# Windowed attention and a token/channel mixer on one core: the last tile's normalised x ahead of a weight conversion's second half, and two parts of u split in one go

## The chip, the core and the metric

The kernel runs on one core of a Trainium2 chip. The metric is the device time of one execution in microseconds (us). Five engines work side by side: TensorE (PE in the profile; PEld is its loading of weights), VectorE (DVE), ScalarE (ACT), GpSimd (POOL) and SyncE (SP), which here does nothing but start transfers. Each engine goes through its own instructions in order; they wait for one another through semaphores. ACT and SP both start DMAs.

## What is computed

Attention in a window of 64 positions, its heads put side by side as x, then a token mixing and a channel mixing with a skip each. All is float32:

```python
# q, k, v: (8, 8, 576, 64)
scores = q @ k^T / 8;  kept where 0 <= row - column < 64, else -1e9
attn   = softmax(scores);  x = (attn @ v) as (8, 576, 512)
h  = relu(x^T @ w_tok1) @ w_tok2        # (576,256), (256,576)
u  = x + h^T
out = u + relu(u @ w_ch1) @ w_ch2       # (512,1536), (1536,512)
```

The weights come as float64.

## The kernel before

**Stages.** The attention stage has 36 tiles, numbered i = 0 to 35 (NT = 36), each with two blocks of 64 rows of all eight heads. For each tile TensorE makes the scores (`qk`), DVE masks them, ACT takes the exponential, TensorE transposes (`pt_transpose`) and multiplies with v (`av`, into the PSUM tile xp), and DVE multiplies xp with the reciprocal sums (`norm`, L355), which gives x of the tile, such as x35. The token mixing is laid between the tiles: `split_x` casts x to a rounded high part xhi on ACT and subtracts to a low part xlo on POOL (L117), `tok1` multiplies both with w_tok1 (into h, L386), `finish_h` and `finish_h_low` make hhi (ACT, L400) and hlo (DVE, L409), and `tok2`, one of the "pieces", makes one of four column parts of u for one of two halves of a batch (up6_1_3 is batch 6, half 1, part 3; L430 and L437). ACT copies each piece from PSUM (L442) into a buffer u (two buffers, u7_1 takes that of u6_1), and after the fourth part a store (L457) brings it to u_dram. The last stores are started by ACT, all others by SP.

After the attention come three stretches of the channel mixing over nine chunks of 512 tokens. The first, on chunk 0, multiplies u with w_ch1 (`gemm1`, PSUM tile gp, L667). `load_u` loads u of a chunk from u_dram (tile uf, L124); for chunk 0 these are four loads on SP, one for each part. `split_u` makes of each part uhi on ACT (L114) and ulo on DVE (L117). One gp tile is twelve products of 512 columns, three for each part of u.

**The weights.** A job is the conversion of a float64 piece of a weight of 384 columns to float32 in DVE's integer arithmetic. `job_convert_a` issues its first half on DVE (L215, L217, L218, tile c). `job_convert_b` issues the second half: L227 and L229 on DVE, then L230 into tile r (one buffer), and one addition on POOL (L232) into tile w (two buffers). For the pieces of w_ch2 that are converted in the attention stage `job_finish` then stores w to w2_dram on SP (L270). Tile 35 has two jobs, 29 and 30.

**What sets the order.** Nothing is rescheduled: each engine's row is the order in which the Python code issues. The table JOBS gives the number of jobs of each tile, PIECES the number of pieces before and behind `av`. In tile 35 the loads of chunk 0's u are issued at the end, behind the stores of the last two jobs. Iteration 36 holds tok1 of x35 and two pieces; the loop over the four parts of u behind it runs the last eight pieces, of batch 7, two with each part. At the end the pieces go in turn to the PSUM tags "up" (one bank), "s" and "pt" (two banks each); "s" and "pt" are gp's tags too.

Of the kernel before, what the change touches and what calls it, by code (L numbers as in the profile page):

```python
# [28 lines left out]
NT = NPAIR * TPP  # L29
DT = 256  # L30
F = 1536
NCT = C // P
# [16 lines left out]
N_START = 7  # L49
# [46 lines left out]
def mixer_kernel(ctx: ExitStack, tc: tile.TileContext, qh, kh, vh, wt1, wt2, wc1, wc2, out):  # L96
# [15 lines left out]
    def split(eng_hi, eng_lo, hi, lo, src):  # L112
        if eng_hi is nc.scalar:
            nc.scalar.copy(hi, src)  # L114
        else:
            eng_hi.tensor_copy(hi, src)
        eng_lo.tensor_sub(lo, src, hi.bitcast(F32))  # L117
# [9 lines left out]
    def split_u(u, cts=range(NCT)):  # L127
        uf, uhi, ulo = u
        for ct in cts:
            split(nc.scalar, nc.vector, uhi[:, ct], ulo[:, ct], uf[:, ct])  # L130
# [5 lines left out]
    with ExitStack() as actx:  # L136
# [8 lines left out]
        def load_k(i):  # L145
            p, t = divmod(i, TPP)
            if t in (0, 4):
                b = 2 * p + (t == 4)
                kbs[b] = pq.tile([P, NBLK + 1, H // 2, BLK], F32, name=f"k{b}", tag="k", bufs=2)
                if b != 0:  # L150
                    nc.sync.dma_start(kbs[b], kh[b])

        def load_q(i):
            qr = pq.tile([P, H // 2, 2, BLK], F32, name=f"q{i}", tag="q", bufs=5)
            nc.sync.dma_start(qr, qh[i])
            loaded[i] = [qr, None]

        def load_v(i):
            vt = pq.tile([P, 2, H, D], F32, name=f"v{i}", tag="v", bufs=3)
            nc.sync.dma_start(vt, vh[i])  # L160
            loaded[i][1] = vt
# [102 lines left out]
        def job_finish():  # L264
            if to_finish:
                n, w = to_finish.pop(0)
                finished.add(n)
                src, hi, lo, o, m = jobs[n]
                if hi is None:
                    nc.sync.dma_start(w2_dram[:, o:o + m], w)  # L270
                else:
                    eng = nc.vector if n >= N_FIRST else nc.gpsimd
                    split(nc.scalar, eng, hi[:, o:o + m], lo[:, o:o + m], w)
                    if src is wt1 and o + m == 5 * DT:
                        for c, r in enumerate((top, bottom)):
                            nc.gpsimd.tensor_copy(t1z[r, c], t1lo[r, 4 * DT:].bitcast(F32))
# [24 lines left out]
        def softmax(i, part):  # L301
            if part == 0:
                st[i] = (pa.tile([P, H], F32, name=f"nm{i}", tag="nm", bufs=3),
                         pa.tile([P, H], F32, name=f"sum{i}", tag="sum", bufs=3))
            nm, sm = st[i]
            mk = mask[1 if tile_blocks(i)[0][1] == 0 else 0]
            for u, h in heads(i, part):
                if (i, u) not in e_sb:
                    e_sb[i, u] = pa.tile([P, 4, P], F32, name=f"e{i}_{u}", tag="e", bufs=4)
                g = 2 * h + u  # L310
                nc.vector.tensor_tensor_reduce(out=e_sb[i, u][:, h], in0=s_ps[i][h // 2 * 2 + u][:, h], in1=mk,  # L311
                                               scale=-scale, scalar=MAX_F32, op0=ALU.add, op1=ALU.min,
                                               accum_out=nm[:, g:g + 1])
# [8 lines left out]
        def pt_transpose(i, u):  # L322
            pp = ps.tile([P, 4, P], F32, name=f"pp{i}_{u}", tag="pt")
            e = e_sb.pop((i, u))
            for h in range(4):
                nc.tensor.transpose(pp[:, h], e[:, h], ident)  # L326
            pt = pa.tile([P, 4, P], F32, name=f"pt{i}_{u}", tag="ptsb", bufs=4)
            nc.scalar.copy(pt, pp)  # L328
            return pt
# [13 lines left out]
        def recip(i):  # L343
            _, sm = st.pop(i)
            ri = pa.tile([P, H], F32, name=f"ri{i}", tag="ri", bufs=2)
            if i < N_START:
                nc.gpsimd.tensor_scalar_add(ri, sm, 1e-9)
            else:
                nc.vector.scalar_tensor_tensor(out=ri, in0=sm, scalar=1e-9, in1=sm, op0=ALU.add, op1=ALU.max)
            nc.vector.reciprocal(ri, ri)  # L350
            return ri
# [98 lines left out]
        def store_u():  # L450
            while stores:
                us, g0, n = stores.pop(0)
                a = 0
                while a < n:
                    j, o = divmod(g0 + a, CHUNK)
                    m = min(n - a, CHUNK - o)
                    (nc.sync if g0 < (B - 1) * S - 320 else nc.scalar).dma_start(u_dram[j][:, :, o:o + m], us[:, :, a:a + m])  # L457
                    a += m
# [16 lines left out]
        def run_pieces(k):  # L475
            for _ in range(min(k, len(pieces))):
                tok2(*pieces.pop(0))
# [23 lines left out]
        for i in range(-1, NT + 1):  # L501
            if 0 <= i and i + 2 < NT:
                load_v(i + 2)
            if 3 <= i + 3 < NT:
                load_q(i + 3)
            if i + 4 < NT:
                load_k(i + 4)
            store_u()
            n_jobs = JOBS[i]
            if i == NT - 1:  # L510
                up_tags += [("s", 2), ("pt", 2)]
            have = len(pieces)
            n_pieces = PIECES.get(i, (1, 1) if i >= TOK2_FROM else (0, 0))
            pts = []
            if 0 <= i < NT:
                pts.append(pt_transpose(i, 0))
                if i < NT - 1:
                    pts.append(pt_transpose(i, 1))
            if i + 1 < NT:
                softmax(i + 1, 0)  # L520
            if i + 1 < NT:
                softmax(i + 1, 1)
            if 0 <= i < NT:
                ri = recip(i)
            if i >= N_START:
                while to_finish:
                    job_finish()
            for n in tok1_plan.get(i + 1, ()):
                last_use = n - NX + ((n - NX) % TPP == 4)
                if n < i and last_use not in tok1_plan.get(i, ()):  # L530
                    split_x(n)
            if i + 1 < NT:
                softmax_exp(i + 1, 0)
            while to_finish:
                job_finish()
            run_pieces(min(have, n_pieces[0]))
            have = min(have, len(pieces))
            if i >= N_START:
                for _ in range(n_jobs):
                    job_convert_a()  # L540
            if i == NT - 1:
                pts.append(pt_transpose(i, 1))
            if i < N_START:
                softmax_exp(i + 1, 1)
            late = i - 1 if i in BEHIND else NT
            for n in tok1_plan.get(i, ()):
                if n < late:
                    tok1(n)
            if N_START <= i < NT - 1:
                softmax_exp(i + 1, 1)  # L550
            if i >= N_START:
                for _ in range(n_jobs):
                    job_convert_b()
            if i == 0:
                job_convert_a()
            if 0 <= i < NT:
                norm(i, av(i, pts), ri)
            finish_h_low()
            if i < N_START:
                for _ in range(n_jobs):  # L560
                    if i > 0:
                        job_convert_a()
                    job_convert_b()
            if i + 2 < NT:
                qk(i + 2)
            if late in tok1_plan.get(i, ()):
                tok1(late)
                finish_h_low()
            if to_convert and N_ABS <= to_convert[0][0] < N_APART and JOBS[i + 1]:
                job_abs()  # L570
            for n in tok1_plan.get(i + 1, ()):
                if n not in xhl:
                    split_x(n)
            run_pieces(min(have, n_pieces[1]))
            while to_load and len(to_convert) < 2 and i < NT - 1:
                job_load()
            if i == NT - 1:
                while to_convert or to_convert_b or to_finish:
                    job_convert_a()
                    job_convert_b()  # L580
                    job_finish()
                qctx.close()
                pu = uctx.enter_context(tc.tile_pool(name="pu", bufs=1, side="right", reuse_waits="tile"))
                ul = {0: load_u(0, pu)}
        for ct in range(NCT):
            split_u(ul[0], (ct,))
            run_pieces(2)
        assert not pieces

# [708 lines left out]
```

## Time and profile before

| | us |
|---|---|
| median of 3 runs | 794.13 (793.02 to 794.43) |
| the profiled execution's own time | 792.06 |
| its span, from the first to the last instruction | 790.3 |
| TensorE busy within the span | 776.4 (98%) |
| DVE, ACT, POOL busy | 591.4, 403.8, 340.2 |

The span lies 1.8 us under the execution's own time; what lies around it is start and end. The granted clock of TensorE was 1.00 in the whole span. A row of a timeline reads: start, duration, engine, line, operation, output and inputs, shapes, and in brackets how long the engine stood idle before it and what ended that. A row of the chain reads: start, duration, what the end of the program hung on in that time.

### The profile page before, as it was taken

The page shows a single profiled execution, that of the slowest core. Times are in us where ns is not written, and L with a number is a line of the kernel's source. Part 1 is how long each engine was busy: PE and PEld are TensorE (multiplying, and loading weights), DVE is VectorE, ACT ScalarE, POOL GpSimd, SP SyncE. Part 2 cuts the span into 40 slices and gives each one's busy share as a digit, 9 for nine tenths or more (in the row PEclk, how much of TensorE's full clock was granted, in tenths as well). Part 3 has the DMA queues.
Part 4 walks back from the last instruction along what each step waited for, and adds up shares of the span by engine and source line. Part 5 has one row for each costly group of instructions (what it writes and reads, how often), then busy time and mean ns, then how long its engine had stood idle before and what let it go on. Part 6 is the DMA issues. An engine that isn't in the chain of part 4 may idle for free.

```text
span 790.3 us, 15910 instructions
## 1 busy us (share of the span) xinstructions
PE 776.4 (98%) x5713; PEld 647.6 (82%) x5713; DVE 591.4 (75%) x1547; ACT 403.8 (51%) x1151; POOL 340.2 (43%) x298
## 2 busy tenths in 40 slices
PE   8999999999999999999999899999999999999997
PEld 6778888888888888888888688888888888888886
DVE  6998889689883987777897866667766667757576
ACT  7999979989864532454425332234323144414040
POOL 4654445444331001025758631549722648723140
PEclk9999999999999999999999999999999999999999
DMA  9866769767847669994979575765975856955533
GB/s 348 309 238 231 240 212 311 257 208 275 280 142 243 191 196 291 287 291 153 304 237 367 197 304 202 264 244 176 330 273 187 294 186 238 345 197 200 199 152 107
DMA packets 88976, 191.76 MB, mean 243 GB/s; under 512 B 9024, under 2 KB 52800, under 8 KB 86976
## 3 DMA queue, kind: packets, MB, share of 16 engines
q1 hardware_dynamic: 86784, 188.90, 69.1%
q10 hardware_dynamic: 2112, 1.84, 0.7%
q8 instruction: 45, 0.74, 0.4%
q14 instruction: 35, 0.29, 0.1%
HBM read 148.24 MB, written 42.47 MB: 241 GB/s over the span
## 4 chain that ended last, share of the span: by engine, by line
PE 66%; DVE 2%; DMA 1%; issue 1%; ACT 0%; POOL 0%; DVEq 0%; POOLq 0%; ACTq 0%
PE op L1109 22%; PE gp L1047 21%; PE gp L667 12%; PE op L675 4%; DMA u_dram<-u 1%; DVE m L904 0%; PE op-1_0_1_3_5769 L1109 0%; PE op-1_1_1_3_6046 L1109 0%; PE op-1_2_1_2_6335 L1109 0%; PE op-1_2_1_0_6333 L1109 0%; PE op-1_2_1_3_6336 L1109 0%; PE op-1_2_0_2_6259 L1109 0%; PE op-1_2_0_3_6260 L1109 0%; PE op-1_2_0_0_6257 L1109 0%; PE op-1_1_1_2_6045 L1109 0%
## 5 line engine op out<-in xcount | busy, mean ns | idle before, releaser
L1047 PE MATMUL gp<-m,w1hi 128*128 128x512 f32 x504 | 155.3, 389 | 2.7 <-DVE x L1056 2.7
L319 ACT ACTIVATE e<-e,nm 128x128 f32<-128x128 f32 x288 | 112.3, 398 | 4.7 <-DVE nm L311 4.7
L1047 PEld LDWEIGHTS gp<-m,w1hi 128*128 128x128 f32 x504 | 94.5, 188 | 22.7 <-DVE x L1056 3.1
L1047 PE MATMUL gp<-m,w1lo 128*128 128x512 f32 x252 | 98.0, 389 | 0.0
L1098 DVE TENSOR_TENSOR uf<-op,uf 128x512 f32<-128x512 f32 (+1 forms) x91 | 61.9, 683 | 39.7 <-PE op L1109 31.9
L117 POOL TENSOR_TENSOR m7lo<-t3g,m7hi 128x512 fp32r<-128x512 f32 x18 | 23.4, 1300 | 148.9 <-ACT m7hi L114 148.9
L311 DVE CUSTOM_DVE_ANT_0 e<-s,mask 128x128 f32<-128x128 f32 x288 | 63.6, 286 | 10.2 <-PE s L292 10.1
L232 POOL TENSOR_TENSOR w<-r,c 128x384 f32<-128x384 f32 (+1 forms) x31 | 30.9, 995 | 67.1 <-DVE r L230 56.1
L667 PE MATMUL gp<-ulo,w1hi 128*128 128x512 f32 x144 | 56.1, 390 | 0.2 <-DVE ulo L117 0.2
L319 ACT ACTIVATION_READ_ACCUMULATOR e<-e,nm 128x1 f32 x288 | 56.2, 195 | 0.0
L667 PE MATMUL gp<-uhi,w1hi 128*128 128x512 f32 x144 | 56.1, 390 | 0.0
L667 PE MATMUL gp<-uhi,w1lo 128*128 128x512 f32 x144 | 56.0, 389 | 0.0
L1047 PEld LDWEIGHTS gp<-m,w1lo 128*128 128x128 f32 x252 | 47.3, 188 | 9.8
L117 POOL TENSOR_TENSOR xlo<-x,xhi 128x512 fp32r<-128x512 f32 x32 | 41.1, 1285 | 29.0 <-ACT xhi L114 28.7
L1050 ACT COPY x<-gp 128x512 f32<-128x512 f32 x18 | 10.6, 588 | 75.3 <-PE gp L1047 75.3
L338 PEld LDWEIGHTS xp<-v,pt 128*64 128x64 f32 x1152 | 36.7, 138 | 13.5 <-ACT e L319 9.0
L292 PE MATMUL s<-k,q 64*64 64x128 f32 x1152 | 40.8, 275 | 2.8 <-DMA q<-qh 1.6
L437 PE MATMUL up<-t2hi,hhi 128*128 128x320 f32 (+1 forms) x128 | 43.0, 336 | 0.0
L338 PE MATMUL xp<-v,pt 128*64 128x64 f32 x1152 | 41.7, 225 | 1.1 <-ACT pt L328 0.8
L326 PE MATMUL pp<-ident,e 128*128 128x128 f32 x288 | 40.9, 277 | 0.5
L328 ACT COPY pt<-pp 128x512 f32<-128x512 f32 x72 | 38.9, 587 | 2.7 <-PE pp L326 1.1
L437 PE MATMUL up<-t2hi,hlo 128*128 128x320 f32 (+1 forms) x128 | 37.8, 296 | 0.0
(477 smaller groups left out, 2146.7 us busy)
## 6 DMA issues: line engine op xcount, KB each, us to landing
v<-vh SPq DMA_DIRECT2D x36, 512.0 KB, 4.3
w1hi<-w1s SPq DMA_DIRECT2D x18, 896.0 KB, 5.2
w1lo<-w1s SPq DMA_DIRECT2D x18, 896.0 KB, 6.9
w1hi<-w2s SPq DMA_DIRECT2D x18, 896.0 KB, 4.5
w1lo<-w2s SPq DMA_DIRECT2D x18, 896.0 KB, 6.4
raw<-wc SPq DMA_DIRECT2D x32, 384.0 KB, 5.2
q<-qh SPq DMA_DIRECT2D x36, 256.0 KB, 4.9
k<-kh SPq DMA_DIRECT2D x7, 1280.0 KB, 8.3
```

Source lines behind the costliest of these rows:

```text
L117: eng_lo.tensor_sub(lo, src, hi.bitcast(F32))
L292: nc.tensor.matmul(so, qt[r, j, half], kbs[b][r, n:n + 2, j], start=True, stop=True)
L311: nc.vector.tensor_tensor_reduce(out=e_sb[i, u][:, h], in0=s_ps[i][h // 2 * 2 + u][:, h], in1=mk, scale=-scale, scalar=MAX_F32, op0=ALU.ad ...
L319: nc.scalar.activation(e[:, h], e[:, h], AF.Exp, bias=nm[:, g:g + 1], scale=-1.0, accum_out=sm[:, g:g + 1])
L326: nc.tensor.transpose(pp[:, h], e[:, h], ident)
L328: nc.scalar.copy(pt, pp)
L338: nc.tensor.matmul(xp[half * BLK:(half + 1) * BLK, h], pts[h % 2][:, h // 2, half * BLK:(half + 1) * BLK], vt[:, half, h], start=True, sto ...
L437: nc.tensor.matmul(up[:, :n], hx[:, cs], w[:, tt * S + s0:tt * S + s0 + n], start=False, stop=(k == 6), skip_group_check=True)
L667: nc.tensor.matmul(gp, w[:, w1_at(ft, ct)], x[:, ct], start=(k == 0), stop=(k == 3 * NCT - 1))
L1047: nc.tensor.matmul(b[INTO[m]], w[:, at], c[:, h, t], start=(k < 4 and z == y == 0), stop=(z == 1 and y == 2), skip_group_check=True)
L1098: eng.tensor_add(x, y, x)
L1109: nc.tensor.matmul(bank[:, cols], w[:, o:o + P], x[:, cols], start=(i == 0 and y == 0 and m in ("m1", "m6", "m7", "m5")), stop=(i == 1 and ...
```

## The change

Two edits. In the last tile (i = 35) the second half of the conversion jobs is no longer issued ahead of `av` and `norm`; it falls to the loop that already closes the tile, which drains all jobs, so it comes behind x35 and the split of x35. And the fourth part of chunk 0's u is split directly behind the third, ahead of the two pieces that stood between them; the last two pieces come behind both.

```diff
             if N_START <= i < NT - 1:
                 softmax_exp(i + 1, 1)
-            if i >= N_START:
+            if N_START <= i < NT - 1:
                 for _ in range(n_jobs):
                     job_convert_b()
...
-        for ct in range(NCT):
-            split_u(ul[0], (ct,))
+        for cts in ((0,), (1,), (2, 3), ()):
+            split_u(ul[0], cts)
             run_pieces(2)
```

How the rows of the engines move. In the rows the first number of a name is that of the tile or the job, the last one is only a running number. DVE, in tile 35, behind the first halves of jobs 29 and 30:

```order
 L218 TENSOR_SCALAR c30_4382<-c30_4382 128x384
+L355 TENSOR_TENSOR x35_4416<-xp35_4399,ri35_4330 128x512
 L227 SCALAR_TENSOR_TENSOR c29_4378<-raw29_4230,c29_4378 128x384
-L229 TENSOR_SCALAR r29_4399<-c29_4378 128x384
-L230 SCALAR_TENSOR_TENSOR r29_4399<-raw29_4230,r29_4399 128x384
+L229 TENSOR_SCALAR r29_4422<-c29_4378 128x384
+L230 SCALAR_TENSOR_TENSOR r29_4422<-raw29_4230,r29_4422 128x384
 L227 SCALAR_TENSOR_TENSOR c30_4382<-raw30_4321,c30_4382 128x384
-L229 TENSOR_SCALAR r30_4405<-c30_4382 128x384
-L230 SCALAR_TENSOR_TENSOR r30_4405<-raw30_4321,r30_4405 128x384
-L355 TENSOR_TENSOR x35_4428<-xp35_4411,ri35_4330 128x512
+L229 TENSOR_SCALAR r30_4429<-c30_4382 128x384
```

x35 moved from behind six instructions to ahead of them; hlo7_0 and hlo7_1 follow behind r30 in both. POOL, at the same place:

```order
-L232 TENSOR_TENSOR w29_4400<-r29_4399,c29_4378 128x384
-L232 TENSOR_TENSOR w30_4406<-r30_4405,c30_4382 128x384
-L117 TENSOR_TENSOR xlo35_4431<-x35_4428,xhi35_4430 128x512
+L117 TENSOR_TENSOR xlo35_4419<-x35_4416,xhi35_4418 128x512
+L232 TENSOR_TENSOR w29_4423<-r29_4422,c29_4378 128x384
+L232 TENSOR_TENSOR w30_4430<-r30_4429,c30_4382 128x384
```

xlo35 moved past both additions. SP's row is the same before and after, and stands here for what follows the stores of w29 and w30 (this is the changed kernel's):

```order
L270 DMA w2_dram_68<-w29_4423 128x384
L270 DMA w2_dram_68<-w30_4430 128x384
L124 DMA uf0_4440<-u_dram0_73 128x512 x4
L247 DMA raw31_4617<-wc2 128x384
L247 DMA raw32_4619<-wc2 128x384
```

The four loads of chunk 0's u stay behind both stores. ACT at the second edit, before:

```order
L114 CAST uhi0_4441<-uf0_4440 128x512
L442 COPY u7_0_4506<-up7_0_0_4497 128x256
L442 COPY u7_0_4506<-up7_0_1_4508 128x256
L114 CAST uhi0_4441<-uf0_4440 128x512
L442 COPY u7_0_4506<-up7_0_2_4520 128x256
L442 COPY u7_0_4506<-up7_0_3_4530 128x256
L457 DMA u_dram7_80<-u7_0_4506 512x1x64
L457 DMA u_dram8_81<-u7_0_4506 512x1x192
L114 CAST uhi0_4441<-uf0_4440 128x512
L442 COPY u7_1_4554<-up7_1_0_4544 128x320
L442 COPY u7_1_4554<-up7_1_1_4556 128x320
L114 CAST uhi0_4441<-uf0_4440 128x512
```

and in the changed kernel, from the second of these stores on:

```order
L457 DMA u_dram8_81<-u7_0_4506 512x1x192
L114 CAST uhi0_4441<-uf0_4440 128x512 x2
L442 COPY u7_1_4556<-up7_1_0_4546 128x320
L442 COPY u7_1_4556<-up7_1_1_4558 128x320
L442 COPY u7_1_4556<-up7_1_2_4569 128x320
L442 COPY u7_1_4556<-up7_1_3_4580 128x320
```

The fourth cast moved past two copies, and those past it. TensorE's row has the same products in the same order before and after.

## The prediction

> **What bounds the kernel now.** I read the page first (span, busy shares, chain), then the chain in order of time, then the engines' timelines and the DMA issues around the one place where the chain leaves TensorE for long.
>
> ```profile
> span 790.3 us, 15910 instructions
> PE 776.4 (98%) x5713; PEld 647.6 (82%) x5713; DVE 591.4 (75%) x1547; ACT 403.8 (51%) x1151; POOL 340.2 (43%) x298
> PE 66%; DVE 2%; DMA 1%; issue 1%; ACT 0%; POOL 0%; DVEq 0%; POOLq 0%; ACTq 0%
> ```
>
> TensorE is busy for 98% of the span, so a change elsewhere counts only where it opens or closes a hole in TensorE's row. The chain in order of time shows such a hole at the end of the attention stage:
>
> ```profile
> 236.12 1.01 POOL w L232
> ...
> 237.38 1.28 POOL xlo L117
> ...
> 238.70 1.42 PE h L386 x5
> ...
> 241.37 0.43 ACT u L442
> ...
> 241.82 8.69 DMA u_dram<-u
> ...
> 251.34 0.53 ACT uhi L114
> ...
> 251.90 0.70 DVE ulo L117
> ...
> 252.64 30.67 PE gp L667 x134
> 283.31 32.64 PE op L675 x144
> ```
>
> The reader is to see two things. TensorE's tok1 product of the last tile (h, 238.70) was held by POOL's xlo, and xlo stands behind a weight's w. Then TensorE's first channel product (gp) was held by the fourth part of chunk 0's u (uhi, ulo), which ScalarE reached late because two copies ahead of it had to wait for a store. From 252.64 on TensorE runs without a hole for over 60 us, so what is won or lost before it reaches the end one to one; the later stages keep their distance from it, since what they wait for is made from its products.
>
> **Edit 1: x35 ahead of the conversion's second half.** The rows of DVE, TensorE, ACT and POOL at that place:
>
> ```profile
> 234.09 1.15 PE L338 MATMUL xp<-v,pt 128*64 128x64 f32 x32
> 233.59 0.55 DVE L227 SCALAR_TENSOR_TENSOR c<-raw,c 128x384 int32<-128x384 int32 x1
> 235.03 0.36 DVE L229 TENSOR_SCALAR r<-c 128x384 int32<-128x384 int32 x1 [0.89 <-POOL w L232]
> 235.43 0.56 DVE L230 SCALAR_TENSOR_TENSOR r<-raw,r 128x384 f32<-128x384 uint32 x1
> 235.91 0.68 DVE L355 TENSOR_TENSOR x<-xp,ri 128x512 f32<-128x512 f32 x1
> 236.68 0.62 ACT L114 CAST xhi<-x 128x512 fp32r<-128x512 f32 x1 [3.29 <-DVE x L355]
> 233.81 1.19 POOL L232 TENSOR_TENSOR w<-r,c 128x384 f32<-128x384 f32 x1 [3.26 <-DVE r L230]
> 236.12 1.01 POOL L232 TENSOR_TENSOR w<-r,c 128x384 f32<-128x384 f32 x1 [1.12 <-issue]
> 237.37 1.28 POOL L117 TENSOR_TENSOR xlo<-x,xhi 128x512 fp32r<-128x512 f32 x1 [0.24 <-ACT xhi L114]
> 237.65 0.40 PE L386 MATMUL h<-xhi,t1hi 128*128 128x512 f32 x1
> ```
>
> xp35 is there at 234.09 + 1.15 = 235.24, and x35 began only at 235.91, behind r30. With x35 first it begins at about 235.28, 0.63 earlier; xhi35 follows at 236.05, xlo35 on POOL (0.69 behind xhi, as before) from 236.74 to 238.02, and the waiting product h at 238.06 instead of 238.70. That is 0.64 us gained at this point. The first h product, at 237.65, does not move, and little of the hole is left behind it.
>
> Now what went behind x35. Two jobs (29 and 30) each have L227, L229 and L230 on DVE, one w on POOL and one store on SP. DVE starts job 29's L227 at 235.94, and its L229 runs from 236.50 to 236.86. L230 then meets xlo35 on POOL (from 236.74). What this costs, two older rows show:
>
> ```profile
> 77.84 1.20 POOL L117 TENSOR_TENSOR w1lo<-w,w1hi 128x384 fp32r<-128x384 f32 x1 [0.95 <-ACT w1hi L114]
> 78.21 1.25 DVE L227 SCALAR_TENSOR_TENSOR c<-raw,c 128x384 int32<-128x384 int32 x1
> ```
>
> A DVE instruction of L230's form, 0.55 alone, took 1.25 beside a POOL subtraction and ended 0.42 after it (79.46 against 79.04). So L230 ends at 238.02 + 0.42 = 238.44, 1.0 later than free. [...]
>
> From there: w29 starts 0.13 after r29 (235.99 to 236.12 in job 30's rows), at 238.57, and takes 1.19 as it did beside job 30's L227: 239.76. r has one buffer, so job 30's L229 waits for w29, as its bracket (0.89) shows, and w30 starts 1.09 after that L229 (235.03 to 236.12): 240.88, ending at 241.89. Before, w30 ended at 237.13. It is 4.76 later.
>
> DVE's hlo7, now behind r30 in DVE's row, would begin at 240.7 instead of 240.11; it costs TensorE a few tenths ahead of the larger wait below and is swallowed by it.
>
> **What stands behind w30 on SP.** Its store to w2_dram, and behind the store the four loads of chunk 0's u:
>
> ```profile
> 237.16 0.33 SPq L270 DMA_DIRECT2D w_dram<-w  x1
> 237.54 0.42 SPq L124 DMA_DIRECT2D uf<-u_dram  x1
> 241.44 1.62 SPq L247 DMA_DIRECT2D raw<-wc  x3
> uf<-u_dram SPq DMA_DIRECT2D x1, 256.0 KB, 3.8
> ```
>
> SP issues in order, so the first load moves from 237.54 to 242.30. The edit that hastens x35 delays data that the last copies stand behind. The landing has no row at its new place. The lower bound is the load's own row, 3.8, taken when little else moved. The upper one comes from a load that ran beside the 640 KB store of ACT:
>
> ```profile
> raw<-wc SPq DMA_DIRECT2D x1, 384.0 KB, 4.9
> u_dram<-u ACTq DMA_DIRECT2D x1, 640.0 KB, 8.7
> u_dram<-u ACTq DMA_DIRECT2D x1, 640.0 KB, 3.5
> ```
>
> The first two are neighbours (the first of SP's three raw loads at 241.44, and the store at 241.82), the third is the last such store, with less beside it. Now the 8.7 us store goes out at about 241.18, 0.64 earlier, and the loads of u come at 242.30, beside its larger part. I take the middle of 3.8 and 4.9, 4.35: the first part of u lands at 246.65. [...]
>
> **Who waits for uf.** ACT's row, and TensorE's:
>
> ```profile
> 242.52 0.62 ACT L114 CAST uhi<-uf 128x512 fp32r<-128x512 f32 x1 [0.73 <-ACT u L442]
> 244.17 0.37 ACT L442 COPY u<-up 128x256 f32<-128x256 f32 x1
> 246.80 0.62 ACT L114 CAST uhi<-uf 128x512 fp32r<-128x512 f32 x1 [1.33 <-issue]
> 246.11 0.38 PE L430 MATMUL up<-ident,x 128*128 128x128 f32 x2
> 249.72 0.39 PE L667 MATMUL gp<-uhi,w1hi 128*128 128x512 f32 x1
> 253.22 0.39 PE L667 MATMUL gp<-uhi,w1hi 128*128 128x512 f32 x1
> 255.95 0.39 PE L667 MATMUL gp<-uhi,w1hi 128*128 128x512 f32 x1
> ```
>
> The first uhi did not wait for uf before (its bracket names ACT's own copy). Now ACT stops at it until 246.7. Behind it on ACT stand the copies of up7_0_0 to up7_0_2. The bank "up" has one buffer; up7_1_1 (246.11 on TensorE) takes it after up7_0_2, whose copy ended at 244.17 + 0.37 = 244.54: 1.57 us of slack. Now that copy ends 2.02 after the first uhi's start (242.52 to 244.54): 248.72, and up7_1_1 starts at 248.76, 2.65 late. All three products up to gp are late by that.
>
> **Edit 2: the fourth part with the third.** The first gp group took from 249.72 to 253.22, 3.50; the next took 2.73 (to 255.95). The 0.77 between them is the wait for the fourth uhi and ulo. With both casts together, the fourth uhi no longer stands behind two copies that wait for the store. The third uhi starts at most 2.63 behind the copy of up7_0_2 (244.17 to 246.80), by 250.98, so the fourth ulo is done by 253.0 (two casts of 0.62, then 0.7); it is needed after ten products of 0.23, at 252.37 + 2.3 = 254.6. The 0.77 goes. The four copies of up7_1 (0.4 each) come behind both casts, until about 253.8; the second gp group, which takes the bank of up7_1_0, starts at 255.1, so they are covered. Without that cover they would cost a cast's length, 0.6.
>
> **Sum.** +2.65 − 0.77 = +1.88 us: 0.64 is won at h, lost at the bank, and the loss is larger than both wins. By the ends of the landing, +1.3 (3.8) to +2.4 (4.9). The profiled execution (792.06, span 790.3) would take 793.9; the median of the runs lies 2.07 above it, at 794.13, which gives 796.0.
>
> **Rivals.**
> 1. Small cost: L230 gets by before xlo35, or the loads land at 3.8. w30 then ends about 0.7 earlier, and the two together leave +0.3 to +1.3. For it: L229 and xlo35 start only 0.24 us apart. Against: L230 comes after xlo35's start by my times, and POOL's rows never let it go early. Time 794.4 to 795.4.
> 2. Not slower: the late loads don't reach TensorE. It decides at the bank "up": if the first part lands by about 244.0 (246.11 less 2.02, and a little), no copy holds up7_1_1 and both wins stay: −0.64 − 0.77 = −1.4, so 792.7. The load would have to land within 1.7 us of its issue, or w30 would have to end by 239.8. The rows of SP and POOL speak against it.
> 3. Heavier contention: the loads and the store meet in full. The raw loads behind the first took longer (a row below); at 6.9 the sum is +4.4, 798.5; at the store's own 8.7 it is +6.2.
>
> ```profile
> raw<-wc SPq DMA_DIRECT2D x1, 384.0 KB, 6.9
> ```
>
> Against it: raw moves half as much again, and the three raw loads themselves now wait.
>
> **How the numbers follow.** 0.2%, 1.59 us, is about what a measurement of this kernel can tell from no change (its runs span 793.02 to 794.43). Late loads as summed 0.60, two thirds of it above 1.59 (0.40 slower, 0.20 same); small cost 0.16 (same); not slower 0.10 (0.04 of it beyond −1.59 with the runs' spread, else same); heavier contention 0.14 (slower). Slower 0.54, same 0.42, faster 0.04. The likeliest case is 796.0, its own range 795.4 to 796.5. The range goes from the small cost's 794.4 less the 1.1 by which a run lies under the median, 793.2, to 798.6, the 6.9 us landing: it leaves out the full gain and the far tail.
>
> **What would show it.** Right: x35 ahead of L227 on DVE, h with next to no wait for xlo, L230 stretched to over 1 us, w30 ending near 241.9, SP's uf loads from about 242.3, the first uhi waiting for DMA uf, TensorE waiting for ACT's u copy ahead of an up product by 2 to 3 us, and no wait for ulo within gp. Wrong: uf loads issued ahead of 240, or no hole of TensorE between 240 and 250; or TensorE's later stages taking the shift up, if one of them is held by something that did not move.

## The result: slower, by more than twice the forecast

The changed kernel takes 798.77 us (median, 798.58 to 799.0), the kernel before on the same chip 793.58 (791.45 to 794.43): a ratio of 1.0073, 95% interval 1.0054 to 1.0091, or +5.2 us. Forecast were 796.0 and +1.9. The place, the sign and the chain of waits are those of the prediction; the size is not, and one cause, TensorE's clock, was not in it. The profiled execution took 799.0, its span is 797.2 (before 790.3).

The chain of the changed kernel in order of time, at the end of the attention stage:

```profile
240.74 1.01 POOL w L232
...
241.76 0.33 SPq L270
...
242.14 5.76 DMA uf<-u_dram
...
248.51 0.64 ACT u L442 x2
249.15 0.52 ACT uhi L114
249.66 0.28 ACT u L442
249.94 0.04 issue
249.99 0.55 PE up L430 x3
250.54 1.12 PE up L437 x6
251.66 0.64 PE up L430 x3
252.30 1.60 PE up L437 x6
...
255.41 32.66 PE gp L667 x144
...
452.27 15.51 PE gp L1047 x60
```

It no longer passes through xlo35 and the store of u. It passes through the second addition w30, that weight's store on SP, the first load of chunk 0's u behind it, ACT's copies behind the first cast, and only then TensorE. Two things in it were not in the forecast. The load takes 5.76, not 4.35. And two equal pieces of TensorE's work (three L430 and six L437 each) take 0.55 + 1.12 and then 0.64 + 1.60. The second is slower although it waits for nothing.

TensorE's timeline at the hole shows why; the bracket is the idle time ahead of a row:

```profile
245.95 0.31 PE L437 MATMUL up<-t2hi,hlo 128*128 128x320 f32 x1
249.99 0.44 PE L430 MATMUL up<-ident,x 128*128 128x128 f32 x2 [3.73 <-ACT u L442]
...
250.67 0.31 PE L437 MATMUL up<-t2hi,hlo 128*128 128x320 f32 x1
250.81 0.31 PE L437 MATMUL up<-t2hi,hhi 128*128 128x320 f32 x1
...
252.90 0.47 PE L437 MATMUL up<-t2hi,hhi 128*128 128x320 f32 x1
253.16 0.47 PE L437 MATMUL up<-t2lo,hhi 128*128 128x320 f32 x1
...
255.25 0.39 PE L667 MATMUL gp<-uhi,w1hi 128*128 128x512 f32 x1
...
258.00 0.39 PE L667 MATMUL gp<-uhi,w1hi 128*128 128x512 f32 x1
```

Right behind the hole like products start 0.14 apart, from about 251.2 to 254.2 they start 0.26 apart, and then 0.15 again. The three pieces behind the hole take 5.26 (249.99 to 255.25); the kernel before needed 3.61 for them (246.11 to 249.72). So 1.65 us are lost besides the hole itself. The table by stages shows it as the granted clock (PEclk); the slow stretch is about the first 2 us of the 32 in the first row. Its rows give start and end, length, busy time of PE, PEld, DVE, ACT and POOL, PEclk, DMA share and GB/s. First the changed kernel, then the kernel before:

```profile
252.00:284.00 32.00, 32.00 (x144) 27.03 (x143) 23.24 (x47) 15.14 (x31) 0.00 (x0) 0.96 0.56 183
452.00:456.00 4.00, 3.73 (x9) 2.98 (x10) 1.74 (x4) 0.64 (x2) 0.00 (x0) 0.57 0.01 2
```

```profile
252.00:284.00 32.00, 31.78 (x139) 26.10 (x140) 27.20 (x54) 16.86 (x33) 0.00 (x0) 1.00 0.48 154
452.00:456.00 4.00, 4.00 (x20) 3.30 (x19) 3.29 (x6) 2.63 (x6) 3.60 (x3) 1.00 0.91 289
```

The second row is a place that the prediction did not speak of: chunk 1's first group, where TensorE waits for DVE's x in every profile. The waits of the changed kernel (us in total, times, longest):

```profile
PE up L430 <- ACT u L442: 3.7, 1, 3.7
PE gp L1047 <- DVE x L1056: 3.0, 1, 3.0
```

The second is 2.7 in the kernel before, and no clock was lost behind it in that execution: the 60 products behind it took 13.89, against 15.51 here.

**Account of the spans (+6.9).** The second gp group starts at 258.00 instead of 253.22: +4.78. The wait near 447 is 0.3 longer, the products behind it take 1.62 longer; the rest, about 0.2, is spread. The executions profiled happen to be a quick one of before (792.06) and a usual one of after; by the medians it is +5.2, and the experiments say how that divides.

Below, "the lag" is the start of the second gp group less the start of the last tile's xp (L338): 253.22 − 234.09 = 19.13 before, 258.00 − 233.90 = 24.10 after. It leaves out what happened ahead of the place. All ratios are to the kernel before on the same chip.

### The profile page after: what moved, and what is told of

The parts are those of the page before. It is cut to its first block, busy times and chain, and to the rows that moved or that the text cites. A ratio compares the mean times of both kernels' runs of the same rounds, so it can differ in the third digit from the quotient of the medians.

```text
span 797.2 us, 15908 instructions
## 1 busy us (share of the span) xinstructions
PE 780.1 (98%) x5713; PEld 650.9 (82%) x5713; DVE 591.9 (74%) x1547; ACT 404.0 (51%) x1151; POOL 339.6 (43%) x298
## 4 chain that ended last, share of the span: by engine, by line
PE 66%; DVE 2%; DMA 1%; issue 1%; ACT 0%; POOL 0%; DVEq 0%; SPq 0%; ACTq 0%
PE op L1109 22%; PE gp L1047 21%; PE gp L667 12%; PE op L675 4%; DMA uf<-u_dram 1%; PE up L437 0%; DVE m L904 0%; PE op-1_0_1_3_5769 L1109 0%; PE op-1_2_1_2_6335 L1109 0%; PE op-1_1_1_3_6046 L1109 0%; PE op-1_2_1_3_6336 L1109 0%; PE op-1_2_0_2_6259 L1109 0%; PE op-1_2_0_3_6260 L1109 0%; PE op-1_2_0_0_6257 L1109 0%; PE op-1_1_1_0_6043 L1109 0%
## 5 line engine op out<-in xcount | busy, mean ns | idle before, releaser
L338 PEld LDWEIGHTS xp<-v,pt 128*64 128x64 f32 x1152 | 36.7, 138 | 13.5 <-ACT e L319 9.0
L437 PE MATMUL up<-t2hi,hhi 128*128 128x320 f32 (+1 forms) x128 | 43.4, 339 | 0.0
L338 PE MATMUL xp<-v,pt 128*64 128x64 f32 x1152 | 41.7, 225 | 1.2 <-ACT pt L328 0.9
L437 PE MATMUL up<-t2hi,hlo 128*128 128x320 f32 (+1 forms) x128 | 38.5, 301 | 0.3 <-DVE hlo L409 0.3
```

Of the source, the lines that this page charges most:

```text
L338: nc.tensor.matmul(xp[half * BLK:(half + 1) * BLK, h], pts[h % 2][:, h // 2, half * BLK:(half + 1) * BLK], vt[:, half, h], start=True, sto ...
L437: nc.tensor.matmul(up[:, :n], hx[:, cs], w[:, tt * S + s0:tt * S + s0 + n], start=False, stop=(k == 6), skip_group_check=True)
```

## The experiments

My theory: the whole loss comes from edit 1, by way of w30's store ahead of the loads of u on SP; it is the late landing and one loss of the clock behind the hole. The rivals: the two edits add up, each with a part; or the stretched subtraction and the hole's neighbours matter more than the loads.

**Edit 1 alone, edit 2 alone.** From the changed kernel, then from the kernel before:

```diff
-        for cts in ((0,), (1,), (2, 3), ()):
-            split_u(ul[0], cts)
+        for ct in range(NCT):
+            split_u(ul[0], (ct,))
```

```diff
-        for ct in range(NCT):
-            split_u(ul[0], (ct,))
+        for cts in ((0,), (1,), (2, 3), ()):
+            split_u(ul[0], cts)
```

> The first edit alone: x35 ahead of the conversion's second halves, the four parts of u split one by one as before. Theory (the late loads of u make the whole loss): about 798.8 us, as the full change, since by the time the first part of u lands the store that the copies of up7_1 wait for is long done and the fourth cast no longer stands behind a wait; TensorE waits about 3.7 us for the copy of up7_0_2 and no more than 0.2 us for ulo. Rival (the two edits add up, as the prediction summed them): 0.8 us more than the full change, 799.6, with the 0.77 us hole for ulo inside the first gp group still there.

> The second edit alone: the fourth part of u split behind the third. Theory: the hole of 0.77 us in the first gp group goes and nothing else moves, so 0.8 us less than the kernel before (0.999 of it). Rival (the copies of up7_1, now behind both casts, come too late for the second gp group): no gain, or up to 0.6 us more.

Edit 1 alone: 798.41 (797.16 to 801.31), ratio 1.0081 (1.0065 to 1.0097). Edit 2 alone: 792.91 (791.34 to 795.1), ratio 1.0002 (0.999 to 1.0013). Edit 1 alone has the whole loss. Its wait, and its chain:

```profile
PE up L430 <- ACT u L442: 3.5, 1, 3.5
242.83 5.47 DMA uf<-u_dram
```

Its lag is 24.73. Its first gp group takes 2.74, with no wait for ulo: the hole ahead of it had covered the fourth part's delay already, so beside edit 1 edit 2 has nothing to win. Without edit 1 the hole within the first gp group does go:

```profile
249.57 0.39 PE L667 MATMUL gp<-uhi,w1hi 128*128 128x512 f32 x1
252.32 0.39 PE L667 MATMUL gp<-uhi,w1hi 128*128 128x512 f32 x1
```

2.75 for the group instead of 3.50, lag 18.38 instead of 19.13. That 0.75 does not show in the median, which is taken up below. Nor does this execution alone show that edit 2 took the wait away: the store that the copies wait for took 7.9 us here, and with 7.8 (before_warm, below) the old order has a group of 2.75 too.

**Filling the hole.** The changed kernel with 14 products that nobody reads, between the products of up7_1_0 and up7_1_1. They keep TensorE busy and shorten nothing:

```diff
-            run_pieces(2)
+            run_pieces(1)
+            if cts == (2, 3):
+                warm = ps.tile([P, C], F32, name="warm", tag="av", bufs=1)
+                for _ in range(14):
+                    nc.tensor.matmul(warm, t2hi[:, :P], t2hi[:, :C], start=True, stop=True)
+            run_pieces(1)
```

> The full change with 14 extra products of 512 columns (0.23 us each, 3.2 us) put into TensorE's row ahead of up7_1_1, into a bank that nothing reads; they compute nothing that is used. Theory (after an idle stretch of 3.7 us the clock is granted at about half speed, which costs 1.65 us of slow products behind the hole): the products behind the hole keep 0.15 us spacing, the granted clock from 250 to 256 is 1.00, and the time falls by 1.6 us to about 797.1, though the wait for the copy ends as late as before. Rival (the products behind the hole are slow for another reason, such as the DMA traffic beside them): no gain, 798.8, and slow products still.

796.26 (795.36 to 798.93), ratio 1.0057 (1.0039 to 1.0075). The rows:

```profile
246.07 3.36 PE L592 MATMUL warm<-t2hi 128*128 128x512 f32 x14
249.79 0.44 PE L431 MATMUL up<-ident,x 128*128 128x128 f32 x2 [0.36 <-ACT u L443]
253.45 0.39 PE L673 MATMUL gp<-uhi,w1hi 128*128 128x512 f32 x1
```

TensorE still waits for the same copy, and up7_1_1 starts as late as in the changed kernel, but the three pieces now take 3.66 (249.79 to 253.45) instead of 5.26, and the lag is 22.33 instead of 24.10. So the 1.65 behind the hole is the clock: with 0.36 of idle time ahead of these pieces, instead of 3.73, it was not lost in this execution. The six executions fall into two groups: 795.36, 795.47 and 795.53 with a mean granted clock of 1.0, and 797.0, 798.77 and 798.93 with 0.995 or 0.996. Something else still took the clock in half of them.

**The stores behind the loads.** The changed kernel, but the stores of w29 and w30 go to SP behind the loads of u (their tiles in a pool of their own, as the old one is given up there):

```diff
-                while to_convert or to_convert_b or to_finish:
+                while to_convert or to_convert_b:
                     job_convert_a()
                     job_convert_b()
-                    job_finish()
                 qctx.close()
...
                 ul = {0: load_u(0, pu)}
+                while to_finish:
+                    job_finish()
```

> The full change with the stores of the weights w29 and w30 to w2_dram issued behind the four loads of u on SP instead of ahead of them (w29 and w30 get buffers in another pool for it). Theory (the loss comes from SP's order alone): the loads of u leave before 240 as in the kernel before, the wait for the copy of up7_0_2 is gone, both wins stay, less about 0.5 us for hlo7 which still stands behind r30: 0.8 to 1.4 us less than the kernel before, about 792.5. Rival (the conversion's delay on DVE and POOL itself costs the time, or the loads wait for their buffers as long): no better than 796.

793.5 (791.0 to 794.77), ratio 1.0011 (1.0 to 1.0022). The first uhi on ACT waits for its own copy again, as in the kernel before, and no longer for a DMA:

```profile
241.83 0.62 ACT L115 CAST uhi<-uf 128x512 fp32r<-128x512 f32 x1 [0.70 <-ACT u L443]
```

x35 is as early and w30 as late as in the changed kernel. What was moved is the order on SP, and with it the loss goes. This shows the step "what stands behind w30 on SP". The gain that I expected beyond it (0.8 to 1.4) does not show: a miss in that part. The lag is 18.55, against 19.13 in the kernel before, but before_warm, below, has 18.36 without either edit. From xp on, the product pieces behind h start 0.6 earlier than in before_warm, but the first piece that needs hlo7, which stands behind r30, takes that and 0.2 more: up7_0_1 starts 8.19 behind xp, against 7.99. That costs more than the 0.5 that I had put for hlo7.

**Less beside the loads.** The changed kernel, but the 640 KB store of u6_1 is started by SP behind the four loads, not by ACT ahead of them:

```diff
-  (nc.sync if g0 < (B - 1) * S - 320 else nc.scalar).dma_start(...)
+  (nc.sync if g0 <= (B - 1) * S - 320 else nc.scalar).dma_start(...)
```

> The full change, with the 640 KB store of u6_1 issued by SP behind the four loads of u instead of by ACT ahead of them. Theory (the loads land in 5.8 instead of 3.8 us because they share the DMA engines with this store): the first part lands within 3.8 to 4.2 us of its issue, the wait for the copy of up7_0_2 shrinks from 3.7 to about 2.0 us, which is too short to lose the clock there, and the time falls by 3.3 us to about 795.4. Rival (the landing is long for another reason): 5.8 us and 798.8 as before.

795.6 (794.6 to 796.7), ratio 1.0033 (1.002 to 1.0046). The issues (KB each, median us to landing), first of the changed kernel, then of this one, and this one's first load and wait:

```profile
uf<-u_dram SPq DMA_DIRECT2D x4, 256.0 KB, 5.6
u_dram<-u ACTq DMA_DIRECT2D x1, 640.0 KB, 3.6
```

```profile
uf<-u_dram SPq DMA_DIRECT2D x4, 256.0 KB, 4.4
242.00 3.69 DMA uf<-u_dram
PE up L430 <- ACT u L442: 1.7, 1, 1.7
```

Issued at the same time (242.00 against 242.14), the first load lands after 3.69 instead of 5.76, the hole shrinks from 3.7 to 1.7, and the lag to 20.47. Behind the hole the three pieces take 3.66 (247.80 to 251.46), so no clock is lost there. So 2.07 of the landing is the store beside it, and the time came out as expected.

**The hazard removed at its root, and a filling near 447.** Four kernels bear on the two open points: what the rearrangement gives if the loads are not delayed, and the second loss of the clock. "best" has both edits, but keeps the second half of job 29 ahead of x35, and the stores of w29 and w30 stand behind the loads as above. "best_warm" adds 11 products that nobody reads ahead of the wait near 447, and "before_warm" is the kernel before with these alone:

```diff
-            if N_START <= i < NT - 1:
-                for _ in range(n_jobs):
+            if i >= N_START:
+                for _ in range(n_jobs if i < NT - 1 else 1):
                     job_convert_b()
```

```diff
+                if n == 0 and m == "m3":
+                    warm = ps.tile([P, CHUNK], F32, name="warm", tag="av", bufs=1)
+                    for _ in range(11):
+                        nc.tensor.matmul(warm, w1hi[:, o - P:o], comb[q, "m7"][:, 0, 1], start=True, stop=True)
```

> Both edits, with two things mended: job 29's second half stays ahead of x35 (DVE is idle there anyway) and only job 30's goes behind it, and the two stores to w2_dram stand behind the loads of u on SP. Theory: x35 at about 235.3 and h 0.6 us earlier, hlo7 not held, no wait for the copy of up7_0_2 and none for ulo: the second gp group starts 17.8 us after the last tile's v products, where the kernel before has 19.13. That is 1.3 us less in executions with the same granted clock (about 790.3 where the kernel before has 791 to 792.5), and 0.998 of the median if the clock is lost as often. Rival (the weights' later stores now hold the first loads of w2 and so the plain stage): no gain.

> The same as best, with 11 extra products (2.5 us, into a bank that nothing reads) in TensorE's row at the wait of 2.7 to 3.0 us near 447, ahead of the first m3 product; they compute nothing that is used. Theory (whether the clock falls after that wait is chance, and it costs 1.6 to 2 us when it does): every execution shows clock 1.000, the spread narrows to about 1 us, and the median is about 790, 0.996 of the kernel before. Rival (the spread between executions comes from something else): spread and clock as in best, and up to 0.2 us more for the extra products.

> The kernel before with the same 11 extra products near 447 and nothing else. Theory: clock 1.000 in every execution, median about 791.6 against 793.2, 0.998. Rival: 793.2 and the same spread.

| | us (range) | ratio, interval | lag |
|---|---|---|---|
| best | 793.14 (790.37 to 795.0) | 0.999 (0.9979 to 1.0002) | 17.79 |
| best_warm | 791.2 (790.81 to 791.41) | 0.9972 (0.9961 to 0.9982) | 17.79 |
| before_warm | 792.11 (790.96 to 792.87) | 0.9984 (0.9976 to 0.9993) | 18.36 |

best has its x35 early, its loads early and the shortest lag of all, 1.34 under the kernel before (0.57 under before_warm, which had no wait for ulo), and its time cannot be told from that of the kernel before. In its profiled execution the clock was lost near 447: the 60 products there took 15.53. With the filling they do not:

```profile
443.13 2.65 PE L1050 MATMUL warm<-m,w1hi 128*128 128x512 f32 x11
445.98 0.73 PE L1054 MATMUL gp<-m,w1hi 128*128 128x512 f32 x2 [0.20 <-DVE x L1063]
```

All executions of both filled kernels have a mean granted clock of 0.999 or 1.0, and best_warm's seven lie within 0.6 us, where the kernel before spread over 3.6 in the same comparison (791.6 to 795.18). The forecast medians, 790 and 791.6, were too low by 1.2 and 0.5. The filling's gain is shown. For the rearrangement itself the intervals of the two ratios overlap, but the executions side by side speak for a gain: all seven of best_warm lie at 791.41 or below, nine of the eleven of before_warm above it. The medians differ by 0.91, the lags by 0.57. One comparison of 7 with 11 executions carries that, so I call it likely and not shown.

**Both fillings together, and edit 2 with the clock held.** after_warm2 is the changed kernel with the 14 and the 11 products; e2_warm is edit 2 alone with the 11; before_warm_b is before_warm once more, beside them on the same chip.

> The changed kernel with both fillings: 14 products in TensorE's hole ahead of up7_1_1 and 11 more ahead of the first m3 product of chunk 1 (near 447); both write a PSUM tile that nothing reads. Theory (the loss is the late landing of u, plus one clock loss behind the hole, plus one by chance near 447, 1.6 each): the hole's filling alone gave 795.4 in the executions with a granted clock of 1.000 and 797.0 to 798.9 in the others; with the second wait filled too all executions should be near 795.4, clock 0.999 or more, the second gp group 22.3 behind xp35, ratio to before about 1.002. Rival (the clock is lost in other places also): the spread to 798 to 799 stays, and the trace shows a granted clock below 1 away from 447.

> The kernel before with the second edit (fourth part of u split with the third) and the 11 products near 447, which compute nothing that is used. Theory A (the wait of 0.77 for the fourth ulo within the first gp group stands in most executions of the kernel before, and a chance clock loss of 1.6 hid its removal): 0.75 below the kernel before with those products alone, so 791.3 against 792.1. Theory B (the wait stands only in some executions): 791.8 to 792.2, no difference that can be told. In both the first gp group takes 2.75.

> The kernel before with the 11 products near 447 (they compute nothing that is used), on the same chip as the second edit with them: 792.1, as it had. Theory A: its trace shows the wait for the fourth ulo, first gp group 3.5. Theory B: it may show 2.75, as it did in the one execution profiled so far.

| | us (range, executions) | ratio, interval | lag |
|---|---|---|---|
| after_warm2 | 795.62 (795.3 to 796.79, 12) | 1.0023 (1.0009 to 1.0038) | 22.36 |
| e2_warm | 791.71 (791.15 to 792.61, 12) | 0.9977 (0.9964 to 0.999) | 18.38 |
| before_warm_b | 792.02 (790.88 to 795.34, 13) | 0.9978 (0.9967 to 0.9988) | 20.42 |

after_warm2 did what the theory said: the group at 797 to 799 is gone, all twelve have 0.999 or 1.0. That divides the result. With the clock held the change costs 795.62 − 792.02 = 3.60. The fillings are worth 798.77 − 795.62 = 3.15 to the changed kernel, and 793.65 − 792.02 = 1.63 to the kernel before (its median in that comparison was 793.65), so clock losses add 1.5. That 3.60 and 1.5 give 5.1 is no check of the split, since the same medians stand in both terms; the check is that the changed kernel's profile shows two losses, 1.65 and 1.62, where the fillings are worth 3.15. The 798.77 is from the first comparison, where the kernel before had 793.58, and each of these differences is known to about 1 us, by the intervals of the ratios.

For edit 2 neither theory was right as I had put it: 791.71 lies between A's 791.3 and B's 791.8, and the medians differ by 0.3. What differs is the spread, 1.5 against 4.5. The profiled execution of before_warm_b is the long one, 795.34. Its chain and TensorE's rows in the first and second gp group:

```profile
242.08 9.99 DMA u_dram<-u
253.47 0.50 PE L668 MATMUL gp<-uhi,w1hi 128*128 128x512 f32 x1 [1.26 <-ACT uhi L115]
254.20 0.50 PE L668 MATMUL gp<-ulo,w1hi 128*128 128x512 f32 x1 [0.23 <-DVE ulo L118]
...
256.16 0.63 PE L668 MATMUL gp<-ulo,w1hi 128*128 128x512 f32 x1
256.59 0.63 PE L668 MATMUL gp<-uhi,w1lo 128*128 128x512 f32 x1
```

The store of u6_1, for which ACT's copies ahead of the fourth uhi wait, took 9.99 here (8.69 in the profile that I predicted from). The first group took 4.79 (249.98 to 254.77) instead of 2.73, and behind it products started 0.43 apart instead of 0.23: the clock was lost in this hole too, for another 1.6. In the other profiled execution of the same kernel (before_warm) the store took 7.8 and had landed in time, and the group took 2.75 (249.88 to 252.63). So the wait that edit 2 takes away was 0, 0.77 and 2.06 in three executions of the same order of work. By its order of work edit 2 cuts this tail, and none of its twelve lies above 792.61; but one long execution among the 24 of the filled kernel before is too few to show it or to put a price on it.

## Why the prediction failed, step by step

- **x35 first, h early.** Right. x35 starts 0.05 behind the end of xp35, and h waits next to nothing for xlo (L386 is not among the waits). The 0.6 won there is gone again at hlo7, a little further on: up7_0_1 starts 8.18 behind xp, against 8.01 before. The forecast had put "a few tenths" for it; as forecast, the larger wait behind it hides this.
- **L230 behind xlo35, w30 late, SP late.** Right to 0.2 us. The rows of DVE, POOL and SP, each from its engine's timeline:

```profile
236.68 1.60 DVE L230 SCALAR_TENSOR_TENSOR r<-raw,r 128x384 f32<-128x384 uint32 x1
236.57 1.29 POOL L117 TENSOR_TENSOR xlo<-x,xhi 128x512 fp32r<-128x512 f32 x1 [6.23 <-ACT xhi L114]
240.74 1.00 POOL L232 TENSOR_TENSOR w<-r,c 128x384 f32<-128x384 f32 x1 [1.12 <-issue]
242.14 2.85 SPq L124 DMA_DIRECT2D uf<-u_dram  x4
```

  L230 starts 0.11 behind xlo35 and ends 0.42 behind its end (238.28 against 237.86), the very figure taken from the older rows. w30 ends at 241.74 (forecast 241.89), and the first load goes out at 242.14 (242.30). The 0.7 that the small cost takes off, should L230 get by, is an estimate that no run shows: with xlo35 just ahead of it L230 took 1.60 here and 1.53 in best.
- **The landing.** Right place, wrong size, and the first of the two terms that failed: the first load took 5.76, the forecast 4.35, the middle of 3.8 and 4.9. That is 1.41 too little. The upper end was taken from another kind of load, beside a slower store (8.7, where it now took 3.6); it is no bound. "Heavier contention", with 6.9 and a chance of 0.14, was the nearer case. Without that store beside it the load took 3.69.
- **The bank "up".** Right. The wait is there with the releaser named, and up7_1_1 starts 3.88 late by the clock of the trace (249.99 against 246.11), 4.07 from xp35 on; the forecast with a landing of 5.76 would have been 2.65 + 1.41 = 4.06.
- **Edit 2: 0.77 saved.** Half right. Beside edit 1 the wait goes away, whether edit 2 is there or not, so for this sum it made no difference. Taken as a property of the kernel before it was a misreading: the wait was 0, 0.77 and 2.06 in three executions.
- **"All three products up to gp are late by that", and no more.** This is the second term that failed, and the sum had none for it. I moved a row of products as a block and kept its durations. Behind a hole of 3.7 they take 5.26 instead of 3.61. No row of the profile of before showed this at that place: the clock was 1.00 throughout in that execution, with a wait of 2.7 near 447 in it. That this wait cost nothing there was the luck of one execution, and the prediction gave the clock neither a term nor a chance.
- **The sum.** With the measured landing the forecast's own sum is +1.88 + 1.41 = 3.29. With the clock held the lag grew by 22.36 − 19.13 = 3.23, or by 4.00 from before_warm's 18.36, and the time by 3.60. So of the 3.3 by which the forecast fell short, 1.41 is the landing and about 1.5 the clock: 1.65 behind the hole here (with edit 1 alone, hole 3.5, the three pieces took 6.18, 2.57 more than before), and the chance of a loss near 447, less what the kernel before loses of its own. One slip in the prediction's numbers changes nothing here: by its own terms the small cost's lower end is 1.88 − 0.7 − 0.55 = +0.6, not +0.3.

Left open: why the granted clock is lost behind a wait of 2.67 to 2.69 near 447 in some executions (best, 15.53; store_sp, 15.43) and not behind one of 2.66 to 2.68 in others (13.89 in the profiles of before, e2_only and behind), and behind one of 3.0 in the changed kernel and with edit 1 alone, but not in the profiled execution of the filled hole (13.90). The length of the wait alone does not decide it in these profiles: behind the waits of 1.26 and 0.23 in before_warm_b the clock was lost, behind the one of 1.7 in store_sp it was not. What does decide it, no run here shows.

## What to carry to other kernels

Before a step is moved behind a critical one, follow what its last instruction issues: here a small store of a weight stood ahead of four loads on the same queue, and the 0.64 us won on TensorE cost five. Holes of 3.5 and 3.7 us in TensorE cost themselves and another 2.6 and 1.65 for the clock here, so a forecast across such a hole must not keep the durations behind it. A wait of 2.7 or 3.0 cost the clock in four of eight profiled executions, and such waits are worth filling with products that nobody reads (0.9984 and 0.9978 here; 0.9972 with the loads kept early, the lowest ratio of all that ran). One profile of before is one execution: a wait that hangs on a DMA's landing should be read from several before its removal is booked as a gain.

## What the hardware showed that I had not expected

- Behind an idle stretch of 3.73 us TensorE first ran on at full pace for about 1 us, then at 0.26 instead of 0.15 per product for 3 (granted clock 0.52 from 252.0 to 254.5), then full again. The loss is 1.65 at the end of the attention stage and 1.62 near 447. It is not always of that size: with edit 1 alone, behind 3.46 us, the products were slow from the first on, for about 5.4 us, and the loss was 2.57.
- The spread of the kernel before is mostly this clock: in its comparison with after_warm2 its seven quickest executions (791.65 to 792.24) have 0.999 or 1.0, and of the seventeen slowest (793.44 to 798.19) only one has more than 0.998. With eleven useless products twelve of thirteen executions (before_warm_b) lie between 790.88 and 793.0, the thirteenth at 795.34.
- The same 640 KB store took 3.6 us in the changed kernel and 7.8, 8.7 and 10.0 in three executions of the old order of work; the same 256 KB load took 3.7 to 5.8, by what else moved.
